# All input products and attention first, then the two later products as seven block products each

## The chip, the cores and the metric

The kernel runs on one core of a Trainium2 chip. The metric is the device time in microseconds (us) of one execution. Three runs of the kernel before took 407.26, 409.66 and 410.86 us; the median is 409.66.

## The reference, cut to what matters

Attention runs in chunks of 32 queries over a window of 16 keys to the left and 8 to the right plus 8 memory slots. Its output x goes through a gated layer:

```python
h = np.maximum(x @ w_in, 0.0)              # x: 4 x 768 x 512, w_in: 512 x 1024
u, v = h[..., :512], h[..., 512:]
v_n = (v - mean(v)) / np.sqrt(var(v) + 1e-6)
v_s = einsum('ts,bsd->btd', w_spatial, v_n) + b_spatial[None, :, None]   # w_spatial: 768 x 768
out = (u * v_s) @ w_out                    # w_out: 512 x 512
```

There are 4 batches of 768 tokens, 8 heads of 64. The host hands over w_in and w_out as 64-bit floats, which the kernel converts.

## The kernel before, in words

**Precision.** Every operand of a large product is held as a high part (rounded to fp32r) and a low part (the rest). A product is three matmuls: high by high, low by high, high by low (`group`, lines 478 to 480). All three add into one PSUM bank.

**Units.** A batch's 768 tokens are 6 attention units of 128 tokens (24 in all). For a unit, `burst` does 64 small matmuls for the scores and 64 for the weighted values (L342), DVE takes the maximum, subtracts and sums (L395, L399, L409), ScalarE (ACT) does the exponential (L404), TensorE (PE) turns the weights and the result (L426, L441), and ACT and DVE write x in two parts (L446, L450).

**The layer.** Three units make a half batch. For each half, `ffn_v` multiplies 3 token tiles by the v half of w_in (12 matmuls of 512 columns each) and normalises them: ACT relu, DVE statistics, GpSimd (POOL) power, DVE scaling, then ACT and DVE split the result. `ffn_u` makes 4 tiles of u (12 matmuls of 384 columns each). `spatial` multiplies by w_spatial: 8 groups per batch, each 18 matmuls of 384 columns, then DVE adds the bias (L577), POOL multiplies by u (L581), ACT and DVE split (L584, L588). `ffn_o` multiplies by w_out: 6 groups of 12 matmuls of 512 columns per batch, ACT copies (L613), SP stores.

**Order.** Every piece is an `op` of a class `Plan` with an engine, an estimated time, reads, writes and a rank. `Plan.order` simulates the engines with these estimates and writes down one fixed order for each engine; at run time each engine works through its order and waits on semaphores. In the kernel before, the attention of batch b+1 lies beside the products of batch b; DMA loads go out on SP's queue as soon as their buffer is free. At the start, `keep_warm` (L493) issues 12 matmuls of 512 columns whose result is not used.

Of the kernel before, what the change touches and what calls it, by code (L numbers as in the profile page):

```python
# [25 lines left out]
class Plan:  # L26
# [8 lines left out]
    def __init__(self, rings, loose, rate, landing, lat):  # L35
        self.rings, self.loose = rings, loose
        self.rate, self.landing, self.lat = rate, landing, lat
        self.ops, self.writer, self.readers, self.slots, self.newest = [], {}, {}, {}, {}

    def op(self, eng, us, fn, r=(), w=(), rank=0.0, mb=0.0, tail=0.0, after=None, alone=False):  # L40
# [20 lines left out]
        self.ops.append((eng, us, fn, deps, rank, mb, tail, held, begun, alone))  # L61
        return n

    def order(self):
# [8 lines left out]
        pipe = {e: self.landing for e in ENGINES}  # L73
        lone = 0.0
# [6 lines left out]
        out = []  # L81
        while len(out) < len(ops):
            best = None
            for e, ns in waiting.items():
                pick = None
                for n in ns:
                    t = max(free[e], ready[n], free["POOL"] if ops[n][9] else 0.0, lone if e == "POOL" else 0.0)
                    for s in ops[n][7]:
# [13 lines left out]
            _, us, _, _, _, mb, tail, held, _, alone = ops[n]  # L102
# [5 lines left out]
            if alone:  # L108
                lone = t + us
            if mb:  # L110
                pipe[e] = max(pipe[e], t + us) + mb / self.rate
                end[n] = pipe[e] + self.landing
            else:
                end[n] = t + us + tail
            self.start[n] = t
            out.append((t, n))
            for m in users[n]:
                left[m] -= 1
                if not left[m]:
                    ready[m] = max([end[d] + self.lat for d in ops[m][3]] + [self.start[d] for d in ops[m][8]])  # L120
                    waiting[ops[m][0]].append(m)
        return [n for _, n in sorted(out)]

    def emit(self):
        for n in self.order():
            self.ops[n][2]()
# [3 lines left out]
def tile_chunked_attention_gmlp(  # L130
# [30 lines left out]
    HT = S // 2  # L161
    NC = S // CH
# [11 lines left out]
    sizes = {"f": 4, "sx": 1, "pt": 1, "xt": 1, "st": 4, "big": 4, "x": 2, "vn": ST, "u": 2 * ND,  # L174
             "q": 1, "k": 1, "vm": 3, "mv": 1, "kT": 1, "p": 1, "xs": 1, "pT": 1}
    plan = Plan(sizes, {"f", "st", "big"}, rate=0.33, landing=2.0, lat=0.06)
# [11 lines left out]
    def pool(name, **kw):  # L188
# [3 lines left out]
    small = pool("small", bufs=3)  # L192
    sb = {name: pool(name, bufs=sizes[name]) for name in ("st", "big", "x", "vn", "u", "q", "k",
                                                         "kT", "p", "xs", "pT")}
    early_scope = ctx.enter_context(ExitStack())
    early = early_scope.enter_context(tc.tile_pool(name="early", bufs=1))
    ps = {name: pool(f"ps_{name}", bufs=sizes[name], space=PSUM) for name in ("f", "sx", "pt", "xt")}

    win_h = const.tile([P, KT, DF], F32R, name="win_h")
    win_l = const.tile([P, KT, DF], F32R, name="win_l")  # L200
    wsp_h = const.tile([P, ST, S], F32R, name="wsp_h")
    wsp_l = const.tile([P, ST, S], F32R, name="wsp_l")
    bias = const.tile([P, S], F32, name="bias")
    memT = const.tile([P, B, T, M], F32, name="memT")
    NV = sizes["vm"]
    vmain = const.tile([P, T, NV * UC, D], F32, name="vmain")
# [3 lines left out]
    warm = const.tile([P, 1], F32, name="warm")  # L210
    make_identity(nc, ident)
    nc.vector.memset(mhalf, -0.5)
# [9 lines left out]
    def load(dst, src_, w, rank, r=(), eng="SP", slow=1.0, us=0.45, seq=False):  # L222
# [5 lines left out]
        n = op(eng, us, lambda: e.dma_start(out=dst() if callable(dst) else dst, in_=src_), r=r, w=w, rank=rank, mb=mb,  # L228
               after=line.get(eng) if seq else None)
# [12 lines left out]
    def spot(name, g, shape):  # L242

        if (name, g) not in t_:
            if g in (1, 2):
                t_[name, g] = early.tile(shape, F32, name=f"{name}{g}")
            else:
                alloc(name, g, shape, F32)
        return t_[name, g]

    def key(name, g):
        return (name if g not in (1, 2) else "early", g, name)

    def load_qk(g, units=(0, 1), seq=True):
# [9 lines left out]
        ks = key("k", g)  # L264
        load(lambda: spot("q", g, [P, T, 2 * UT])[:, :, q0:q1],
             src(q, off + q0, [[S, P], [P * S, T], [1, q1 - q0]]), w=[key("q", g) + (u,)], rank=10.0 * i, slow=1.3, seq=seq)
        load(lambda: spot("k", g, [P, T, nk])[:, :, k0:k1],
             src(k, off - LEFT + k0, [[S, P], [P * S, T], [1, k1 - k0]]), w=[ks + (u,)], rank=10.0 * i, slow=1.3, seq=seq)
# [10 lines left out]
    def qk_keys(i, names="qk"):  # L279
        g, both = i // 2, [0, 1] if i == 1 else [0]  # L280
        return [key(n, g) + (u, *p) for n in names for u in both for p in ((), ("pad",))]
# [11 lines left out]
    def load_v(i, seq=True):  # L293
        b, c0 = i // UB, (i % UB) * UC
        n = UC
        v4 = v_of(i).rearrange("p t c d -> p t (c d)")
        for r in range(2):
            p0 = r * D
# [4 lines left out]
            def part(dst, src_, s, rows):  # L303
                load(dst, src_, w=[("vm", i, r, s)], rank=10.0 * i, slow=1.5, us=0.35, seq=seq)
# [10 lines left out]
    def v_keys(i):  # L315
        return [("vm", i, r, s) for r in range(2) for s in range(4)] + \
            [("mv", i // UB, r, t) for r in range(2) for t in range(T)]

    def load_mem(b, eng="SP", us=0.3, seq=True):
        for r in range(2):  # L320
            for t in range(T):
                load(vmain[r * D + CH:r * D + SLOT, t],
                     src(mem_v, (b * H + 2 * t + r) * M * D, [[D, M], [0, NV * UC], [1, D]]),
                     w=[("mv", b, r, t)], rank=10.0 * UB * b, eng=eng, slow=1.5, us=us, seq=seq)

    def prep(i, rank):
        b = i // UB

        def keys():
            a = alloc("kT", i, [P, T, UC + 1, SLOT], F32)  # L330
            nc.scalar.copy(a[:, :, :, 0:CH], k_of(i).rearrange("p t (c s) -> p t c s", s=CH))

        def mem():
            nc.gpsimd.tensor_copy(t_["kT", i][:, :, 0:UC, CH:SLOT],
                                  memT[:, b].unsqueeze(2).broadcast_to([P, T, UC, M]))
        op("ACT", act(T * (UC + 1) * CH), keys, r=qk_keys(i, "k"), w=[("kT", i)], rank=rank)
        op("POOL", 0.3, mem, r=["memT", ("kT", i)], w=[("kT", i, "m")], rank=rank)

    def burst(i, rank, split=False):

        def mm(o, w_, m):
            nc.tensor.matmul(o, w_, m, start=True, stop=True, skip_group_check=True)  # L342

        def go(what):
            if ("sx", i) not in t_:
                alloc("sx", i, [P, 2, 2, T, D], F32, psum=True)
            sx = t_["sx", i]
            tiles = [(t, c, r, slice(r * D, (r + 1) * D)) for t in range(T) for c in range(UC) for r in range(2)]
            if "s" in what:
                tq = q_of(i)  # L350
                kT = t_["kT", i].rearrange("p t c s -> p t (c s)")
# [8 lines left out]
        for what in (whole if split else [whole]):  # L360
            reads, writes = [], []
            us = 0.4
            if "s" in what:
                reads += qk_keys(i, "q") + [("kT", i), ("kT", i, "m")]
                writes.append(("sx", i, 0))
                us += 0.6
            if "a" in what:
                reads += [("pT", i - 1)] + v_keys(i - 1)
                writes.append(("sx", i, 1))
                us += 0.7  # L370
# [14 lines left out]
    def softmax(i, rank):  # L385
# [32 lines left out]
        op("DVE", dve(512) + 0.36, den, r=[("p", i)], w=[("rec", i)], rank=rank + 0.6)  # L418

    def flip(i, rank):  # L420
        if i < NU:
# [6 lines left out]
            def copy():  # L428
                nc.scalar.copy(alloc("pT", i, [P, T, P], F32), t_["pt", i])
            op("PE", 0.45, turn, r=[("p", i)], w=[("pt", i)], rank=rank, tail=0.25)  # L430
            op("ACT", act(512) - 0.04, copy, r=[("pt", i)], w=[("pT", i)], rank=rank)
        if i >= 1:
# [19 lines left out]
            op("PE", 0.45, turn_x, r=[("xs", j)], w=[("xt", j)], rank=rank - 0.5, tail=0.25)  # L452
            op("ACT", act(512) - 0.04, high, r=[("xt", j)], w=[("x", n, tt, "h")], rank=rank - 0.5)
            op("DVE", dve(512), low, r=[("xt", j), ("x", n, tt, "h")], w=[("x", n, tt, "l")], rank=rank - 0.5)
# [11 lines left out]
    def group(N, pairs, needs, first=(), get=None):  # L466
# [5 lines left out]
        for j, (pair, keys) in enumerate(zip(pairs, needs, strict=True)):  # L472
            def go(j=j, pair=pair):
# [7 lines left out]
            op("PE", 3e-3 * (0.4375 * N + 6.5), go, r=[*keys, *(first if j == 0 else ())], w=[("f", n)],  # L481
               rank=1e4 + seq[0], tail=0.25)
        seq[0] += 1
        return n

    def keep_warm(c, passes, rank):

        n = ("w", c)

        def go():  # L490
            o = alloc("f", n, [P, DH], F32, psum=True)
            for _ in range(passes):
                nc.tensor.matmul(o, win_h[:, c, DH:DH + P], win_h[:, c, DH:], start=True, stop=True)  # L493
        op("PE", passes * 0.43, go, r=[("win", c, 1, "h")], w=[("f", n)], rank=rank, tail=0.25)
# [4 lines left out]
    def ffn_v(b, tt):  # L499
        n_x, tok = 2 * b + tt // HU, slice((tt % HU) * P, (tt % HU + 1) * P)  # L500
        i = b * ST + tt
        rank = 45 + 1e-3 * seq[0]

        def pair(c):
# [3 lines left out]
                  [[("win", c, 1, s) for s in "hl"] + x_keys(b, tt) for c in range(KT)], [("vn", i)], lambda: alloc("vn", i, [P, 2, DH], F32R))  # L508
# [21 lines left out]
        def high():  # L530
            nc.scalar.copy(t_["vn", i][:, 0], t_["st", s])

        def low():
            a = t_["vn", i]
            nc.vector.tensor_tensor(a[:, 1], t_["st", s], a[:, 0].bitcast(F32), op=ALU.subtract)
        k_ = ("st", s)
        op("ACT", act(512), relu, r=[("f", n)], w=[k_], rank=rank)
        op("DVE", 1.05, stat, r=[k_], w=[("ve", i)], rank=rank)
        op("POOL", 0.6, power, r=[("ve", i)], w=[("rstd", i)], rank=rank)
        op("DVE", 0.43, norm, r=[("rstd", i)], w=[k_], rank=rank, alone=True)  # L540
        op("ACT", act(512), high, r=[k_], w=[("vn", i, "h")], rank=rank)
# [253 lines left out]
```

## Time and profile before

| | |
|---|---|
| median of three runs | 409.66 us |
| profiled execution, span from the first to the last instruction | 410.6 us |
| PE busy | 377.1 us, 92% |
| DVE, ACT, POOL busy | 201.2, 156.2, 99.3 us |
| DMA | 41.03 MB, mean 100 GB/s |

A matmul's time in a group is from its start to its modelled end; neighbours overlap, so the pace is read from the starts of successive matmuls in the timeline. The profile gives TensorE's granted clock in tenths; 1.00 is the upper of its two levels (2.4 GHz), 0.50 the lower (1.2 GHz). The execution that was profiled has no time of its own on the page beside its span.

### The profile page before, as it was taken

How to read it: one execution, taken by the hardware profiler on the slowest of the kernel's cores; microseconds unless marked ns; L12 is line 12 of the kernel's file. 1: busy time of each engine (PE TensorE's matmuls, PEld its weight loads, DVE VectorE, ACT ScalarE, POOL GpSimd, SP SyncE). 2: the span in 40 equal slices, each digit the busy share in tenths (PEclk: the TensorE clock that was granted, in tenths of full speed). 3: DMA queues.
4: the chain of work that ended last, by engine and by line, in shares of the span. 5: the costliest groups of instructions: out<-in, count | busy, mean ns of one | idle time of the engine just before them, and what ended most of it. 6: DMA issues, size and time to landing. Idle time of an engine off the chain costs nothing.

```text
span 410.6 us, 11090 instructions
## 1 busy us (share of the span) xinstructions
PE 377.1 (92%) x4824; PEld 336.2 (82%) x4824; DVE 201.2 (49%) x391; ACT 156.2 (38%) x277; POOL 99.3 (24%) x129
## 2 busy tenths in 40 slices
PE   1394899989999999989999999999999999999996
PEld 0263688879989887969997988989989989899895
DVE  0766787677736625665561631476331414424040
ACT  2645667376343324443424223344221123231212
POOL 5322359338302201011120120110120301103031
PEclk9996699999999999999999999999999999999999
DMA  7997734792343293320377332000002020000202
GB/s 183 249 253 206 237 125 133 199 283 83 85 148 127 57 242 105 92 93 7 106 149 209 116 110 77 2 2 2 3 0 77 2 77 2 0 0 2 77 2 77
DMA packets 35153, 41.03 MB, mean 100 GB/s; under 512 B 5216, under 2 KB 29664, under 8 KB 35104
## 3 DMA queue, kind: packets, MB, share of 16 engines
q1 hardware_dynamic: 34704, 40.05, 34.4%
q8 instruction: 38, 0.62, 0.7%
q0 software_dynamic: 256, 0.20, 0.4%
q14 instruction: 11, 0.09, 0.1%
q10 hardware_dynamic: 144, 0.07, 0.1%
HBM read 34.01 MB, written 6.29 MB: 98 GB/s over the span
## 4 chain that ended last, share of the span: by engine, by line
PE 73%; issue 7%; DMA 7%; DVE 3%; SPq 3%; POOL 3%; ACT 3%; POOLq 0%; ACTq 0%
PE f L478 21%; PE f L479 20%; PE f L480 20%; PE sx L342 7%; DMA big<-in_moe_w_in_dram 5%; SPq L228 3%; PE xt L441 2%; PE pt L426 2%; DMA big<-in_moe_w_out_dram 2%; POOL st L646 1%; DMA q<-in_q_dram 1%; ACT st L631 1%; DVE st L528 1%; ACT big L636 1%; DVE stats L516 0%
## 5 line engine op out<-in xcount | busy, mean ns | idle before, releaser
L478 PE MATMUL f<-wsp_h,vn 128*128 128x384 f32 x192 | 66.7, 348 | 0.0
L479 PE MATMUL f<-wsp_h,vn 128*128 128x384 f32 x192 | 64.7, 337 | 0.0
L480 PE MATMUL f<-wsp_l,vn 128*128 128x384 f32 x192 | 64.6, 336 | 0.0
L581 POOL TENSOR_TENSOR st<-st,u 128x384 f32<-128x384 f32 x32 | 33.2, 1037 | 123.9 <-DVE st L577 119.6
L478 PE MATMUL f<-x,win_h 128*128 128x384 f32 x128 | 44.6, 349 | 0.0
L577 DVE TENSOR_TENSOR st<-f,bias 128x384 f32<-128x384 f32 x32 | 17.8, 556 | 52.6 <-PE f L480 52.6
L479 PE MATMUL f<-x,win_l 128*128 128x384 f32 x128 | 43.2, 338 | 0.0
L480 PE MATMUL f<-x,win_h 128*128 128x384 f32 x128 | 43.2, 337 | 0.0
L584 ACT CAST big<-st 128x384 fp32r<-128x384 f32 x32 | 16.4, 513 | 67.7 <-POOL st L581 67.7
L524 POOL TENSOR_TENSOR rstd<-ve,mhalf 128x1 f32<-128x1 f32 x24 | 15.1, 628 | 111.3 <-DVE ve L520 98.9
L478 PE MATMUL f<-win_h,x 128*128 128x512 f32 x96 | 40.0, 417 | 1.6 <-issue 1.6
L478 PE MATMUL f<-wout,big 128*128 128x512 f32 (+1 forms) x100 | 39.1, 391 | 0.0
L480 PE MATMUL f<-wout,big 128*128 128x512 f32 (+1 forms) x100 | 38.6, 386 | 0.0
L479 PE MATMUL f<-wout,big 128*128 128x512 f32 (+1 forms) x100 | 38.6, 386 | 0.0
L479 PE MATMUL f<-win_h,x 128*128 128x512 f32 x96 | 38.5, 401 | 0.0
L480 PE MATMUL f<-win_l,x 128*128 128x512 f32 x96 | 38.4, 400 | 0.0
L478 PEld LDWEIGHTS f<-wsp_h,vn 128*128 128x128 f32 x192 | 36.1, 188 | 1.4
L479 PEld LDWEIGHTS f<-wsp_h,vn 128*128 128x128 f32 x192 | 36.2, 188 | 0.7
L480 PEld LDWEIGHTS f<-wsp_l,vn 128*128 128x128 f32 x192 | 36.1, 188 | 0.0
L516 DVE BATCH_NORM_STATS2 stats<-st 128x6 f32<-128x512 f32 x24 | 16.5, 689 | 32.8 <-ACT st L512 32.7
L342 PEld LDWEIGHTS sx<-kT,q 64*32 64x32 f32 x1536 | 17.3, 109 | 18.4 <-issue 8.4
L378 DVE TENSOR_TENSOR xs<-sx,rec 128x512 f32<-128x512 f32 x24 | 16.5, 687 | 32.2 <-PE sx L342 28.7
(67 smaller groups left out, 676.2 us busy)
## 6 DMA issues: line engine op xcount, KB each, us to landing
vmain<-in_v_dram SPq DMA_DIRECT2D x48, 128.0 KB
out_dram<-st SPq DMA_DIRECT2D x23, 256.0 KB
q<-in_q_dram SPq DMA_DIRECT2D x11, 512.0 KB
vmain<-in_v_dram SPq DMA_DIRECT2D x47, 96.0 KB
big<-in_moe_w_in_dram SPq DMA_DIRECT2D x8, 512.0 KB
k<-in_k_dram SPq DMA_DIRECT2D x7, 544.0 KB
k<-in_k_dram SPq DMA_DIRECT2D x4, 576.0 KB
big<-in_moe_w_spatial_dram SPq DMA_DIRECT2D x6, 384.0 KB
```

The costliest lines, as they stand in the source:

```text
L228: n = op(eng, us, lambda: e.dma_start(out=dst() if callable(dst) else dst, in_=src_), r=r, w=w, rank=rank, mb=mb, after=line.get(eng) if s ...
L342: nc.tensor.matmul(o, w_, m, start=True, stop=True, skip_group_check=True)
L378: nc.vector.tensor_tensor(xs.rearrange("p t r d -> p r t d"), t_["sx", i][:, :, 1], rec.rearrange("p t r -> p r t").unsqueeze(3).broadcast ...
L426: nc.tensor.transpose(a[:, t], p[:, t], ident)
L478: nc.tensor.matmul(o, lh, rh, start=(j == 0), stop=False)
L479: nc.tensor.matmul(o, ll, rh, start=False, stop=False)
L480: nc.tensor.matmul(o, lh, rl, start=False, stop=(j == len(pairs) - 1))
L516: nc.vector.bn_stats(stats, t_["st", s])
L524: nc.gpsimd.tensor_tensor(a, t_["ve", i], mhalf, op=ALU.pow)
L577: nc.vector.tensor_tensor(alloc("st", s_, [P, HT], F32), t_["f", n], bias[:, tok], op=ALU.add)
L581: nc.gpsimd.tensor_tensor(a, a, t_["u", i], op=ALU.mult)
L584: nc.scalar.copy(t_["g", i][:, 0, 0:HT], t_["st", s_])
```

## The change

What it does:

- **Two halves of the program.** Attention of all batches, `ffn_v` and `ffn_u` come first. The normalised v and u are no longer kept in SBUF: each tile is stored to buffers in DRAM (`vn_far`, `u_far`). In the second half they are loaded again, batch by batch (`near_v`, `near_u`); the loads of v wait for the end of attention, those of u for the last matmul group of the first half.
- **Seven block products.** `spatial` and `ffn_o` become calls of `product`, which cuts both operands in 2 x 2 blocks and makes seven block products instead of eight. The left operands' sums s1 to s4 are made by DVE for each batch, and each of the seven left operands is split by ACT and DVE. The right operands (w_spatial, w_out) get their seven sums once (`right_hand`). The bias of the first 384 positions enters as one more matmul of a group; POOL adds the difference for the other positions (`shift`). `ffn_o` of a batch runs between the products of the next batch's `spatial`. Its matmuls have 256 columns.
- **DMA.** A transfer is issued only once an older one has landed, so that at most 8 transfers and 1.75 MB (2.0 MB over the first 9 MB) are in flight. The memory values come in two loads and are copied to their places by POOL and DVE. The load order at the start differs.
- **PE.** `keep_warm` is gone; between 9 and 36 us of the plan's time, gaps are filled with matmuls of a constant. The planner's estimates change, one of them for DVE and POOL beside each other.
- **Last stores.** The last block's stores are halved, one half on SP's queue, one on ACT's.

```diff
+    def held_by(self, flight, mb, none):
+        window = self.window if sum(size for _, size in flight) > self.early[0] else self.early[1]
+        for back, (name, size) in enumerate(reversed(flight), 1):
+            mb += size
+            if back == 8 and window == self.window or mb > window:
+                return name
+        return none
...
+    def busy(k):
+        for _ in range(k):
+            nc.tensor.matmul(idle, ident, ident.unsqueeze(1).broadcast_to([P, 2, P]), start=True, stop=True)
...
+        op("SP", 0.45, lambda: transfer(nc.sync, vn_far[i // HU][:, i % HU], t_["st", s], P * DH * 4e-6), r=[k_],
+           w=[("vn_far", i // HU, i % HU)], rank=rank, mb=P * DH * 4e-6)
...
+        load(get, vn_far[i], w=[("vr", i)], r=["attended"] + [("vn_far", i, j) for j in range(HU)], rank=rank)
...
+        load(get, u_far[(b * 2 + dh) * 2 + th], w=[("ug", i, 0), ("ug", i, 1)],
+             r=[("u_far", i, j) for j in range(2)] + [("fin", n) for n in range(count[0])], rank=rank)
...
+    def product(kind, b, steps, halves, chunks, width, parts, N, right, right_keys, sum_eng, seed, done):
...
+                    for s in range(chunks):
+                        h, l_ = half(0)[:, s, cols], half(1)[:, s, cols]
+                        rh, rl = right(bi, 0, s), right(bi, 1, s)
+                        for x, y in ((h, rh), (l_, rh), (h, rl)):
...
+                s1 = total("s1", a21, a22, ALU.add, [*k21, *k22])
+                s2 = total("s2", s1[0], a11, ALU.subtract, [*s1[1], *k11])
...
+            blocks(name, left(*of), i, bank, name in ("p1", "p2", "p5"))
+            yield
...
+            def gate(x, dh, th):
+                u = ("ug", (b, dh, th))
+                def go():
+                    g = t_[u][:, p]
+                    nc.gpsimd.tensor_tensor(g, t_[st(x)], g, op=ALU.mult)
+                op("POOL", 1.3, go, r=[st(x)], w=[(*u, p)], rank=rank)
...
+        return product("s", b, ["p1", "p2", "p6", "p5", "p7", "p4", "p3"], [quarter(0, 0), quarter(0, 1), quarter(1, 0), quarter(1, 1)], HU, 2 * P, 2, HT,
...
+        return product("o", b, ["p1", "p6", "p5", "p7", "p4", "p3", "p2"], [quarter(1, 1), quarter(1, 0), quarter(0, 1), quarter(0, 0)], 2, HT, HU, HN,
...
+    load_mem()
...
     load_qk(0, (0,))
...
+    load_qk(0, (1,))
+    w_in_part(0, 1, 5.0 + 0, 2.0 + 0, "DVE")
+    w_in_part(1, 1, 5.0 + 1, 2.0 + 1, "DVE")
+    w_in_part(2, 1, 5.0 + 2, 2.0 + 2, "DVE")
+    w_in_part(3, 1, 5.0 + 3, 2.0 + 3, "DVE")
     load_v(0)
...
+    load_qk(1)
+    w_in_part(0, 0, 25.0 + 0, 15.0 + 0, "POOL")
     load_v(1)
...
+    w_in_part(1, 0, 25.0 + 1, 15.0 + 1, "POOL")
     load_v(2)
...
+    w_in_part(2, 0, 25.0 + 2, 15.0 + 2, "POOL")
+    w_in_part(3, 0, 25.0 + 3, 15.0 + 3, "POOL")
...
+            spatials.append(spatial(b))
+            for _ in range((1, 2, 2, 1)[b]):
+                next(spatials[b])
+        if b:
+            o = ffn_o(b - 1)
+            if b == B - 1:
+                for _ in range(6):
+                    next(o)
+                held = o
+            else:
+                next(o)
+                if b == B:
+                    for _ in held:
+                        pass
+                for _ in o:
+                    pass
+        if b < B:
+            for _ in spatials[b]:
+                pass
```

## Rows read from the trace of the kernel before

**Rows 1.** The head of the profile page: span, busy time of the engines, and the span in 40 slices of 10.3 us, PE's busy tenths and its granted clock in tenths.

```profile
span 410.6 us, 11090 instructions
PE 377.1 (92%) x4824; PEld 336.2 (82%) x4824; DVE 201.2 (49%) x391; ACT 156.2 (38%) x277; POOL 99.3 (24%) x129
...
PE   1394899989999999989999999999999999999996
...
PEclk9996699999999999999999999999999999999999
```

**Rows 2.** Busy time of each engine in four stretches (us from the start): PE, PEld (weight loads), DVE, ACT, POOL, each with its instructions; then PE's mean granted clock, the DMA engines' mean busy share, and GB/s.

```profile
0.00:50.00 50.00, 26.24 (x519) 19.71 (x523) 27.50 (x53) 24.47 (x41) 16.93 (x30) 0.86 0.89 223
36.00:48.00 12.00, 8.50 (x156) 6.61 (x156) 8.93 (x16) 6.39 (x11) 3.53 (x4) 0.51 0.65 182
50.00:400.00 350.00, 343.71 (x4272) 310.41 (x4272) 172.61 (x338) 129.38 (x231) 81.10 (x99) 1.00 0.28 83
50.00:250.00 200.00, 193.71 (x3191) 172.91 (x3191) 115.36 (x226) 87.82 (x155) 57.39 (x71) 1.00 0.46 131
210.00:220.00 10.00, 10.00 (x172) 8.37 (x171) 5.06 (x10) 2.98 (x6) 2.25 (x3) 1.00 0.99 203
```

**Rows 3.** PE's groups in the first 50 us, with the idle time ahead of each and what ended it: the unused matmuls of L493, and the weighted values of L342.

```profile
L493 PE MATMUL f<-win_h 128*128 128x512 f32 x12 | 5.7, 616 | 6.6 <-ACT win_h L649 6.6
L342 PE MATMUL sx<-vmain,pT 64*32 64x64 f32 x199 | 4.5, 283 | 7.7 <-issue 3.4 <-ACT pT L429 2.5 <-ACT st L631 1.8
```

**Rows 4.** Matmul groups of the whole span, shapes apart; each stands for one of the three lines 478 to 480, so the number of matmuls is three times the count.

```profile
L478 PE MATMUL f<-wsp_h,vn 128*128 128x384 f32 x192 | 66.7, 348 | 0.0
...
L478 PE MATMUL f<-x,win_h 128*128 128x384 f32 x128 | 44.6, 349 | 0.0
...
L478 PE MATMUL f<-win_h,x 128*128 128x512 f32 x96 | 40.0, 417 | 1.6 <-issue 1.6
...
L478 PE MATMUL f<-wout,big 128*128 128x512 f32 x92 | 36.9, 401 | 0.0
```

**Rows 5.** The timeline of PE near the end (start, duration, both in us): 384 columns, 512 columns, and then the first and the last of 15 successive matmuls of 256 columns.

```profile
396.94 0.34 PE L478 MATMUL f<-wsp_h,vn 128*128 128x384 f32 x1
...
397.81 0.34 PE L480 MATMUL f<-wsp_l,vn 128*128 128x384 f32 x1
...
399.21 0.39 PE L478 MATMUL f<-wout,big 128*128 128x512 f32 x1
...
400.38 0.39 PE L480 MATMUL f<-wout,big 128*128 128x512 f32 x1
...
405.16 0.28 PE L478 MATMUL f<-wout,big 128*128 128x256 f32 x1
...
406.84 0.28 PE L480 MATMUL f<-wout,big 128*128 128x256 f32 x1
```

**Rows 6.** The chain that ended last, pieces from 120 to 130 us (start, duration): the small matmuls of one attention unit, and four turns of each kind.

```profile
124.54 0.44 PE pt L426 x4
...
126.03 1.55 PE sx L342 x104
...
129.36 0.44 PE xt L441 x4
```

**Rows 7.** Groups of ACT, POOL and DVE over the whole span: the conversion of w_in, the softmax of a unit, the bias and the low parts.

```profile
L631 ACT ACTIVATE st<-big 128x512 f32<-128x512 f32 x12 | 8.0, 667 | 12.1 <-DMA big<-in_moe_w_in_dram 8.5 <-DMA big<-in_moe_w_out_dram 3.6
L649 ACT CAST win_h<-st 128x512 fp32r<-128x512 f32 x8 | 5.0, 622 | 3.5 <-POOL st L646 3.5
L687 ACT CAST wsp_h<-big 128x768 fp32r<-128x768 f32 x6 | 4.9, 832 | 0.0
L404 ACT ACTIVATE p<-p 128x512 f32<-128x512 f32 x24 | 15.2, 632 | 17.6 <-DVE p L399 17.5
L581 POOL TENSOR_TENSOR st<-st,u 128x384 f32<-128x384 f32 x32 | 33.2, 1037 | 123.9 <-DVE st L577 119.6 <-ACT big L584 4.3
L646 POOL TENSOR_TENSOR st<-st,big 128x512 uint32<-128x512 uint32 x12 | 16.5, 1375 | 32.6 <-DVE st L641 14.1 <-issue 6.4 <-ACT big L636 5.3
L654 POOL TENSOR_TENSOR win_l<-st,win_h 128x512 fp32r<-128x512 f32 x4 | 5.7, 1416 | 3.5 <-ACT win_h L649 2.0 <-DMA q<-in_q_dram 1.5
L577 DVE TENSOR_TENSOR st<-f,bias 128x384 f32<-128x384 f32 x32 | 17.8, 556 | 52.6 <-PE f L480 52.6
L399 DVE TENSOR_TENSOR p<-sx,mx 128x512 f32<-128x512 f32 x24 | 16.5, 689 | 5.9 <-PE sx L342 5.4
L588 DVE TENSOR_TENSOR big<-st,big 128x384 fp32r<-128x384 f32 x32 | 21.7, 679 | 18.4 <-ACT big L584 18.1
```

**Rows 8.** DMA: what was read and written over the span, from the page; and the stretch with hardly anything but a store of 256 KB in it, with the columns of the second group.

```profile
HBM read 34.01 MB, written 6.29 MB: 98 GB/s over the span
...
380.00:390.00 10.00, 10.00 (x50) 8.86 (x49) 0.56 (x1) 2.28 (x4) 0.55 (x1) 1.00 0.21 79
```

**Rows 9.** The last piece of the chain that ended last: the copy out of PSUM ahead of the last store.

```profile
407.15 0.37 ACT st L613
```

**Rows 10.** The timeline of POOL and DVE from 393 to 396 us (start, duration): one product by u, and two low parts, the first beside it and the second alone.

```profile
393.68 1.02 POOL L581 TENSOR_TENSOR st<-st,u 128x384 f32<-128x384 f32 x1 [0.54 <-DVE st L577]
...
393.72 1.39 DVE L588 TENSOR_TENSOR big<-st,big 128x384 fp32r<-128x384 f32 x1
...
395.27 0.56 DVE L588 TENSOR_TENSOR big<-st,big 128x384 fp32r<-128x384 f32 x1 [0.17 <-ACT big L584]
```

More of the change, by code (lines that the diff above doesn't have):

```diff
@@ L60, in op @@
         begun -= deps
-        self.ops.append((eng, us, fn, deps, rank, mb, tail, held, begun, alone))
+        self.ops.append((eng, us, fn, deps, rank, mb, tail, held, begun, alone, drag, shared))
         return n
@@ L101, in order @@
             (t, _, n), e = best
-            _, us, _, _, _, mb, tail, held, _, alone = ops[n]
+            if e == "PE" and self.idle and 9.0 < t < 36.0:
+                spare = int((t - max(free[e], 9.0) - 0.5) / 0.45)
+                if spare > 0:
+                    spares.append((max(free[e], 9.0), -spare))
+            _, us, _, _, _, mb, tail, held, _, alone, drag, shared = ops[n]
+            beside, pace = {"DVE": (free["POOL"] if shared else 0.0, 1.75), "POOL": (both, 1.4)}.get(e, (0.0, 1.0))
+            if beside > t:
+                us += min((beside - t) * (1 - 1 / pace), us * (pace - 1))
             for s in held:
@@ L161, in tile_chunked_attention_gmlp @@
     HT = S // 2
+    HN = H * D // 2
     NC = S // CH
@@ L191, in tile_chunked_attention_gmlp @@
     const = pool("const", bufs=1)
[L192 to L206, printed above, removed]
+    small = pool("small", bufs=8)
+    sb = {name: pool(name, bufs=sizes[name]) for name in ("st", "big", "uo")}
+    ps = {"f": pool("ps_f", bufs=sizes["f"], space=PSUM)}
+    far = pool("far", bufs=1, space=bass.MemoryType.DRAM)
+    vn_far = [far.tile([P, HU, DH], F32, name=f"vn_far{i}") for i in range(2 * B)]
+    u_far = [far.tile([P, 2, HT], F32, name=f"u_far{i}") for i in range(4 * B)]
+    wsp = const.tile([P, 7, 2, HU, HT], F32R, name="wsp")
+    bias = const.tile([P, HT], F32R, name="bias")
+    step = const.tile([P, HT], F32, name="step")
+    ones = const.tile([P, P], F32R, name="ones")
     ident = const.tile([P, P], F32, name="ident")
@@ new lines, in spread_mem, with spread @@
+    def spread_mem(i, eng, rank):
+        b, o = i // UB, (i % NV) * UC
+        for r in range(2):
+            rows = slice(r * D + CH, r * D + SLOT)
+            def spread(rows=rows, r=r):
+                to, of = vmain[rows, :, o:o + UC], memv[rows, b].unsqueeze(2).broadcast_to([M, T, UC, D])
+                ins = {"DVE": nc.vector, "POOL": nc.gpsimd}[eng].tensor_copy(to, of)
+                made.setdefault(("vmem", i % NV), []).append(ins.ins.name)
+            op(eng, 1.1 if eng == "POOL" else 1.25, spread, r=[("memv", r)], w=[("vmem", i % NV, r)], rank=rank)
@@ L480, in go @@
                 nc.tensor.matmul(o, lh, rl, start=False, stop=(j == len(pairs) - 1))
-            op("PE", 3e-3 * (0.4375 * N + 6.5), go, r=[*keys, *(first if j == 0 else ())], w=[("f", n)],
-               rank=1e4 + seq[0], tail=0.25)
+            op("PE", 3e-3 * (0.4375 * N + 6.5), go, r=[*keys, *(first if j == 0 else ())],
+               w=[("f", n), ("fin", n)], rank=1e4 + seq[0], tail=0.25)
         seq[0] += 1
         return n
[L486 to L494, printed above, removed]
     def x_keys(b, tt):
@@ new lines, in second_half, with third_part @@
+    def second_half():
+        if "op" not in sb:
+            attention.close()
+            for name in ("vr", "op", "sm"):
+                sb[name] = pool(name, bufs=sizes[name], side="right")
+            ps["y"] = pool("ps_y", bufs=sizes["y"], space=PSUM, side="right")
+    def third_part():
+        if "ug" not in sb:
+            ffn.close()
+            for name in ("ug", "ot"):
+                sb[name] = pool(name, bufs=sizes[name])
+            t_["wout"] = pool("wout", bufs=1).tile([P, 7, 2, 2, HN], F32R, name="wout")
@@ new lines, in from_f64, with split, high, low @@
+        if home:
+            return (lambda: t_[big][:, :, 1].bitcast(F32)), ("big", big)
+        return (lambda: t_["st", ("z", name)]), zk
+    def split(eng, n, dst, of, reads, writes, rank):
+        def high():
+            nc.scalar.copy(dst(0), of())
+        def low():
+            e = {"POOL": nc.gpsimd, "DVE": nc.vector}[eng]
+            e.tensor_tensor(dst(1), of(), dst(0).bitcast(F32), op=ALU.subtract)
+        op("ACT", act(n), high, r=reads, w=[(*w, "h") for w in writes], rank=rank)
+        op(eng, pool_(n) if eng == "POOL" else dve(n), low, r=[*reads, *[(*w, "h") for w in writes]], w=writes, rank=rank,
+           shared=eng == "DVE")
@@ new lines, in w_out_pair, with halves, dst @@
+    def w_out_pair(c, rank, load_rank):
+        def halves(z):
+            return lambda: z().rearrange("p (h n) -> p h n", h=2)
+        def dst(i, x):
+            third_part()
+            return t_["wout"][:, i, x, c]
+        (zu, ku), (zd, kd) = [from_f64(("wout", d), w_out[d * P:(d + 1) * P], 260.0, load_rank, True) for d in (c + 2, c)]
+        end = [("fin", n) for n in range(count[0])]
+        right_hand("wout", c, HN, halves(zu), halves(zd), [ku, *end], [kd, *end], dst, rank, "POOL", "DVE")
@@ new lines, in load_bias, with relative, high, low @@
+    def load_bias(rank):
+        raw = ("big", "bias")
+        def get():
+            t_[raw] = alloc("big", "bias", [P, 1024], U32).bitcast(F32)
+            return t_[raw][:, 0:S]
+        def relative():
+            nc.gpsimd.memset(t_[raw][:, S:S + P], 0.0)
+            for j in range(2):
+                nc.gpsimd.memset(t_[raw][CH * j:CH * j + 1, S:S + P], 1.0)
+            nc.gpsimd.tensor_tensor(step, t_[raw][:, HT:S], t_[raw][:, 0:HT], op=ALU.subtract)
+        def high():
+            nc.scalar.copy(bias, t_[raw][:, 0:HT])
+            nc.scalar.copy(ones, t_[raw][:, S:S + P])
+        def low():
+            b2 = bias[CH:CH + 1]
+            nc.vector.tensor_tensor(b2, t_[raw][CH:CH + 1, 0:HT], b2.bitcast(F32), op=ALU.subtract)
+        load(get, src(b_sp, 0, [[0, P], [1, S]]), w=[raw], r=[("wsp", 2, 6)], rank=rank, seq=True)
+        op("POOL", 1.6, relative, r=[raw], w=["step", (*raw, "d")], rank=rank)
+        op("ACT", 0.8, high, r=[raw, (*raw, "d")], w=["bias h"], rank=rank)
+        op("DVE", dve(HT), low, r=["bias h", raw], w=["bias"], rank=rank)
@@ new lines, in tile_chunked_attention_gmlp @@
+    for i in range(NU + 1):
+        attend(i, 10.0 * i, 1 <= i < UB)
+        j = i + 2
+        if i >= 1 and j < NU:
+            if j >= UB and j % UB < NK:
+                spread_keys(j, 10.0 * j)
+            if j >= UB and j % UB < NV:
+                spread_mem(j, "POOL", 10.0 * j)
+            load_v(j)
+        if i % 2 == 1 and i // 2 + 2 < NU // 2:
+            load_qk(i // 2 + 2)
+        if i - UB in (0, 4, 8):
+            w_sp_pair((0, 4, 8).index(i - UB), 10.0 * i + 15)
+        if i == UB + 11:
+            load_bias(10.0 * i)
```

529 lines of the change are left out of this document (327 added, 202 removed).

## Prediction

> **What bounds the kernel now.** I read the page's head and its slices first. PE is busy 377.1 of 410.6 us, no other engine over 49%, and PE's digits fall below 8 only in the first five slices [rows 1]. The windows then put numbers on it: from 0 to 50 us PE is busy 26.24 us, from 50 to 400 us 343.71 of 350 [rows 2]. So this is a PE-bound kernel with a poor start, and only two things can shorten it much: fewer PE cycles after 50 us, or a better first 50 us. The start loses 50 − 26.24 = 23.8 us idle, another 5.7 us to matmuls whose result nobody uses [rows 3], and half of the 8.50 busy us between 36 and 48 us, where the granted clock is 0.51, the lower level, after a stretch with gaps [rows 2]: 23.8 + 5.7 + 4.2 = 33.7 us.
>
> **PE's cycles.** Before, the w_spatial product has 3 x 192 = 576 matmuls of 384 columns [rows 4]. Pace from the starts of neighbours: five steps of 384 columns take 397.81 − 396.94, 0.174 us each; five of 512 take 1.17, 0.234 each; fourteen of 256 take 1.68, 0.120 each [rows 5]. After, per batch: 7 products x 2 parts x 3 chunks x 3 = 126, and 2 for the bias; four batches make 512. That is 64 x 0.174 = 11.1 us less. The w_out product has 24 x 12 = 288 of 512 columns (67.4 us); after, 4 x 7 x 3 x 2 x 3 = 504 of 256 (60.5 us): 6.9 us less. PE was never idle in that stage, so all **18.0 us** count. The danger is that a 256-column matmul has a weight load of its own; the fourteen steps were each a new weight load and still held 0.120.
>
> **The start.** Before u can be made, the loads up to the last w_in part must land: memory 0.13 MB, q and k of two units 1.08, w_in for v 2.10, values of three units 1.38, next q and k 1.11, w_in for u 2.10: 7.9 MB. At the 223 GB/s of the first 50 us [rows 2] that is 35.4 us. The last part's conversion then takes two ACT passes, two DVE passes, a POOL addition, an ACT cast and a POOL subtraction; with 0.67 twice, two DVE passes of up to 0.69, 1.38, 0.62 and 1.42 [rows 7] about 6 us. So PE can run dense from about 41 us. By then it has done three attention units at 1.55 + 0.44 + 0.44 = 2.43 us [rows 6], a fourth unit's scores (0.8) and three v tiles of 12 x 0.234 = 2.8: 16.5 us. Loss 24.5 instead of 33.7, a gain of **9.2 us**. Bounds: nothing, if the fillers stand ahead of late data; 13 us, if the loads run at 250 GB/s (223 at a share of 0.89). I take the computed value, as its rate is this stage's own. The fillers count nothing while they lie in idle time; they should hold the clock at its upper level where the rows show 0.51.
>
> **The first half after that** costs nothing by my account, and this is what covers it. Per half batch PE has 3 x 2.43 for attention, 3 x 2.8 for v and 4 x 12 x 0.174 = 8.4 for u: 24 us. One unit's chain is scores 1.55, two DVE passes 0.69, exponential 0.63, turn 0.44, a copy of about 0.6, some 4.6 us; three take 14, so attention stays ahead. DVE's 201.2 us lose in this half the work on spatial (17.8 + 21.7, [rows 7]) and the low part of v (24 x 0.69), leaving 145 us in some 217. POOL gets 32 us for w_spatial's sums and low parts and 30 to 50 us of copies of memory values (no row: bounds 0.3 and 2.4 us each, nearest a POOL pass over 768 elements); its queue is not full. SP gets 48 stores more in line with the loads: a load behind a store waits for that store's ACT or DVE step. What they hold up next is a unit's q, k or v; one half batch of attention ahead is the cover, and a stall here would show as PE idle at the scores.
>
> DMA is the tight one. Read 34.0 MB plus 12.6 MB of stores [rows 8], less 7.9 MB by 41 us, is 38.7 MB until the half ends: PE needs 24 x 2.43 + 288 x 0.234 + 384 x 0.174 = 192.5 us, less 16.5, so 176 us, or 220 GB/s. In 50 to 250 us the engines gave 131 GB/s at a share of 0.46, 285 when full; stores alone 79 at 0.21, 376 [rows 8]; the worst slice 203 at 0.99 [rows 2]. 26 MB at 250 to 285 and 12.6 MB at 376 take 125 to 138 of 176 us. Price: nothing to +15 us (all of it at 203 GB/s: 191 us). I take 0, by the stretch of 200 us rather than the slice of 10.
>
> **The hand-over.** The first v block of the second half needs a load of 0.8 MB, two of them 1.6 MB, after the last unit: 5.8 us at 270, some 3 to land (407.52 to 410.6 is what the last store takes, [rows 1, 9]), then a cast of 0.83 [rows 7] and a low part of 0.95: under 10 us. In line on PE meanwhile is the last v tile and four u tiles: 2.8 + 8.4 = 11.2 us. Cost 0; without that cover 10 us.
>
> **The second half's new work on DVE.** From 0.556 (384) and 0.689 (512) [rows 7] one more element costs 1.04 ns: 768 elements 0.955, 256 elements 0.42. Per batch w_spatial needs 4 sums + 7 low parts at 0.955 and 8 passes at 0.556: 15.0 us; w_out 11 x 0.955 + 9 x 0.42 = 14.3. That is 29.3 us beside 22.3 + 15.1 = 37.4 of PE, 78%. POOL has 10 passes of 1.04 per batch. The trace shows that the two hinder each other: a low part took 1.39 beside POOL's product and 0.56 alone [rows 10]. At 0.83 for every POOL pass DVE comes to 37.6 of 37.4; the mean over 32 (0.679, [rows 7]) says a third to half of it. So PE should stay the bound with short waits where w_spatial and w_out change over and at the end, where w_out's last six products are alone: there p6 waits for a multiply, two sums, a cast and a low part, some 4.3 us behind 3.1 + 2.2 + 2.2 us of PE work. I take **+5 us** (one at each of three changes, two at the end); bounds 0 and 16 (DVE's 150 us and 10 for w_out's preparation in place of PE's 150, and 6 at the changes).
>
> The Trainium skill, in "SBUF — State Buffer", section "Who interferes with whom", says that a DVE instruction with two SBUF inputs and a GpSimd instruction that reads SBUF exclude each other for a whole instruction. The 1.39 agrees. By that rule taken for every pass the sum would carry the upper bound of 16.
>
> **The tail.** An addition of 0.42 replaces a copy of 0.37 [rows 9], and the stores are half as large: 0 within 0.3 us.
>
> **Sum.** 410.6 − 18.0 − 9.2 + 5 = 388.4 us. The median of the three runs lies 0.9 below the span, and a run's time has nothing else shown around it, so I set 387.5.
>
> **Rivals.**
>
> 1. *DVE becomes the bound of the second half.* For it: 37.6 against 37.4 us at the full price of [rows 10], in queues with a fixed order. Against: the mean of 0.679. Time: waits of 16 instead of 5, and half the start's gain: 387.5 + 11 + 4.6 = 403. Range 396 to 408.
> 2. *Slower: DMA bounds the first half.* Place: q, k and v loads in one line with 12.6 MB of new stores, at most 8 in flight. Price: each 10 GB/s below 220 costs about 8 us. Slower than before means 27 us lost, 38.7 MB in 203 us: it decides at 191 GB/s. At 170 GB/s: 228 us, +52, about 439; at 185, 421. For it: a slice at 203. Against: no full slice under 203, 285 over the long stretch. The Trainium skill ("SBUF — State Buffer", "A bandwidth-pool intuition that's wrong (but worth ruling out)") holds HBM to be the usual end-to-end bottleneck; here a mean of 98 GB/s over the span shows that it was not before the change.
> 3. *Weight loads bound the 256-column products.* PEld's loads are shown at 0.188 us; at that pace 504 x 0.068 = 34 us more, 421. Against: fourteen steps at 0.120 [rows 5].
> 4. *Better still.* Start at its upper bound, no waits, and half of the 6.3 us idle in 50 to 400 gone: 387.5 − 3.8 − 5 − 3 = 376.
>
> That the change does less than it says is only possible where an order leaves PE waiting, which is rival 1.
>
> **Chances.** Forecast (378 to 396) 0.70; rival 1 0.12; rival 2 0.08; rival 3 0.03; rival 4 0.07. The range from 376 to 404 holds the forecast, most of rival 1 and half of rival 4, about 0.82. Three runs of before spread over 0.9%, so 1% (405.6 to 413.8) is what counts as no change. Faster: 0.70 + 0.07 + 0.09 of rival 1 = 0.86; same: 0.03 of rival 1, 0.02 of rivals 2 and 3 = 0.05; slower: 0.09.
>
> **What would show it.** PE's cycles: 171 per line of 384 columns from w_spatial and 168 of 256 from w_out, at 0.120 between starts. Start: busy above 30 us of the first 50 without the fillers, clock 1.00 throughout. First half: DMA near 200 GB/s and hardly any PE idle ahead of the small attention matmuls. Second half: DVE about 80% busy, PE waits on its low parts of 5 us together. Wrong would be long PE waits for v loads between 50 and 217 us (rival 2), a pace of 0.188 (rival 3), or DVE above 95% with PE under 90% (rival 1).

## The result, and the profile after

The changed kernel took 376.78 us (median of 4 runs, 375.94 to 377.45) against 408.46 us, a ratio of 0.925 with a 95% interval of 0.9191 to 0.9309. Measured once more beside the experiments it was 376.59 us (6 runs), ratio 0.9239 (0.9211 to 0.9266). 387.5 was forecast, 376 to 404 as the range: the direction was right, the time lies 0.8 us inside the range's lower edge, 11 us under the forecast and below the forecast's own band of 378 to 396. Ratios leave out executions that lie over 1.5% above the fastest of the same kernel.

The head of the page after and its slices of 9.35 us answer to [rows 1]:

```profile
span 374.1 us, 11859 instructions
PE 357.9 (96%) x4996; PEld 329.4 (88%) x4996; DVE 282.5 (76%) x472; ACT 188.8 (50%) x336; POOL 159.4 (43%) x158
...
PE   2998999999989999999999999999999999999996
...
PEclk9999999999999999999999999999999999999999
```

The start fills after one slice, and once the clock is up it does not fall. In the first 13 us the row shows 1.00, but the durations show the lower level: the 64 small matmuls of a unit's scores take 1.18 us there and 0.86 later, both in the changed kernel:

```profile
10.81 1.18 PE L411 MATMUL sx<-kmain,q 64*32 64x64 f32 x64
23.72 0.86 PE L411 MATMUL sx<-kmain,q 64*32 64x64 f32 x64
```

The kernel before has such a stretch too, up to about 24 us (1.18 us for the same 64 matmuls at 6.98 us), where [rows 1] show the upper level. The same kernel in stretches (columns as in [rows 2]): the first 50 us, the rest of the first half, the second half, the end.

```profile
0.00:50.00 50.00, 40.30 (x786) 32.05 (x786) 37.93 (x73) 29.13 (x50) 26.90 (x34) 1.00 0.95 245
50.00:217.00 167.00, 164.76 (x3171) 145.13 (x3171) 114.33 (x237) 85.20 (x150) 70.32 (x79) 1.00 0.69 208
217.00:360.00 143.00, 142.54 (x957) 142.10 (x956) 122.44 (x151) 69.19 (x127) 62.21 (x46) 1.00 0.35 118
360.00:374.10 14.10, 10.35 (x88) 10.12 (x86) 7.83 (x14) 5.29 (x11) 0.00 (x0) 1.00 0.35 112
```

Of the first 50 us the filling matmuls took 11.98:

```profile
0.00:50.00 50.00, 11.98 (x44) 8.94 (x44) 1.00 0.95 245
```

The chain of the second half (start, duration) shows the two paces, each over 18 matmuls, and the last addition ahead of the last stores, which answers to [rows 9]:

```profile
224.94 3.12 PE f L704 x18
...
254.51 2.10 PE f L704 x18
...
370.38 0.42 DVE ot L814
```

Dividing, 3.12 / 18 is 0.1733 us for 384 columns, 2.10 / 18 is 0.1167 for 256. Now the 36.5 us between the spans can be split:

| | forecast | measured |
|---|---|---|
| PE's cycles in the two products | −18.0 | −19.7 (0.120 forecast, 0.1167 found) |
| the first 50 us | −9.2 | −12.0 (33.7 lost before; 9.7 idle + 12.0 filler now) |
| PE idle from 50 us to its last matmul | +5 | −3.6 (6.3 before; 2.24 + 0.46 now) |
| after the last matmul | 0 | +0.3 |

That is −35.0. Of the 1.5 us left, some 0.4 are the lower level at the very start, which the table does not count (half of PE's busy time there without the unused matmuls, an estimate, is 1.9 us before and 1.5 now); the rest is not assigned to any row.

The split holds for the two profiled executions. The one of the kernel before was a long one: its span of 410.6 us compares with 404.3 to 411.4 in the 37 other executions of it on record, whose medians on three occasions were 406.3, 407.5 and 408.1. The medians of the times differ by 31.7 us, not 36.5. The prediction took the median to lie 0.9 us below the span; on record an execution takes 1.7 to 2.2 us more than its own span. The second half of the changed kernel hardly varies (149.05 us, and 148.99 when it was run again), so up to 5 us of what the table gives to the start and to idle time may belong to that one execution.

### The profile page after: what moved, and what is told of

Its sections match the earlier page's. It is cut to its first block, busy times and chain, and to the rows that moved or that the text cites. A ratio compares the mean times of both kernels' runs of the same rounds, so it can differ in the third digit from the quotient of the medians.

```text
span 374.1 us, 11859 instructions
## 1 busy us (share of the span) xinstructions
PE 357.9 (96%) x4996; PEld 329.4 (88%) x4996; DVE 282.5 (76%) x472; ACT 188.8 (50%) x336; POOL 159.4 (43%) x158
## 4 chain that ended last, share of the span: by engine, by line
PE 88%; DVE 5%; ACT 2%; issue 2%; DMA 1%; SPq 0%; ACTq 0%; DVEq 0%
PE y L704 22%; PE f L704 15%; PE f L553 12%; PE f L554 11%; PE f L555 11%; PE sx L411 9%; PE xt L515 3%; PE pt L499 3%; DMA k<-in_k_dram 1%; DVE op L682 1%; DVE st L867 1%; PE idle L251 1%; DVE st L866 1%; DVE sm L665 0%; PE y L698 0%
## 5 line engine op out<-in xcount | busy, mean ns | idle before, releaser
L704 PE MATMUL y<-wsp,op 128*128 128x384 f32 x288 | 52.6, 336 | 0.0
L760 POOL TENSOR_TENSOR ug<-st,ug 128x384 f32<-128x384 f32 x24 | 35.8, 1508 | 35.8 <-DVE st L752 31.6
L704 PEld LDWEIGHTS y<-wsp,op 128*128 128x128 f32 x288 | 50.1, 188 | 0.0
L704 PE MATMUL f<-wsp,op 128*128 128x384 f32 x216 | 39.4, 336 | 0.0
L682 DVE TENSOR_TENSOR op<-sm,op 128x768 fp32r<-128x768 f32 x32 | 35.7, 1121 | 4.8 <-ACT op L679 4.6
L704 PEld LDWEIGHTS f<-wsp,op 128*128 128x128 f32 x216 | 37.6, 188 | 0.0
L704 PE MATMUL y<-wout,op 128*128 128x256 f32 x288 | 35.9, 280 | 0.5 <-DVE op L682 0.5
L704 PEld LDWEIGHTS y<-wout,op 128*128 128x128 f32 x288 | 34.8, 188 | 0.9 <-DVE op L682 0.8
L679 ACT CAST op<-sm 128x768 fp32r<-128x768 f32 x32 | 26.3, 839 | 12.7 <-DVE sm L665 9.0
L390 POOL COPY vmain<-memv 8x1024 f32<-8x1024 f32 x22 | 23.5, 1075 | 11.5 <-PE sx L411 9.2
L704 PE MATMUL f<-wout,op 128*128 128x256 f32 x216 | 27.0, 280 | 0.0
```

Of the source, the lines that this page charges most:

```text
L390: ins = {"DVE": nc.vector, "POOL": nc.gpsimd}[eng].tensor_copy(to, of)
L679: nc.scalar.copy(half(0), of())
L682: nc.vector.tensor_tensor(half(1), of(), half(0).bitcast(F32), op=ALU.subtract)
L704: nc.tensor.matmul(o, x, y, start=first and m == 1 and not (seed and bank == "y"), stop=m == 3 * chunks, skip_group_check=True)
L760: nc.gpsimd.tensor_tensor(g, t_[st(x)], g, op=ALU.mult)
```

## The experiments

Ratios are to the kernel before on the same chip; 0.01 of it is 4.1 us. The base is the changed kernel run again among them:

> The changed kernel unchanged, as the base for the other runs: 0.925 of the kernel before, as measured.

0.9239 (0.9211 to 0.9266).

**Does PE's work count one for one?**

```diff
-                    for s in range(chunks):
+                    again = 2 if name == "p2" and kind == "s" else 1
+                    for s in list(range(chunks)) * again:
```

> The changed kernel with the matmuls of the second block product of the w_spatial product done twice (so this product is counted twice in the output): 8 x 9 = 72 more matmuls of 384 columns, the order of all engines the same. My theory, PE bounds the second half and its cycles count one for one: 72 x 0.174 = 12.5 us more, 389 us. Rival, DVE (81% busy there) sets the pace and PE has slack: 0 to 5 us more.

0.9535 (0.9499 to 0.9571): 12.1 us more than the base, 13.5 more by the span (387.6 against 374.1; 12.8 against the base's 374.8). The second half alone shows it best: from the first matmul of the two products to the end of the last one the traces have 149.05 us in the changed kernel, 148.99 when it was run again, and 161.39 here, 12.3 more. One for one. The same line with kind "o":

> The same for the w_out product: its last block product of each batch done twice, 4 x 3 x 6 = 72 more matmuls of 256 columns. My theory: 72 x 0.120 = 8.6 us more, 385 us. Rival 3 of the prediction, weight loads at 0.188 us bound these products: 13.5 us more. Rival, DVE sets the pace where w_out's products run: under 3 us more.

0.9392 (0.9353 to 0.9432): 6.3 us more, give or take 2; by the span (382.6) 7.8 to 8.5. The second half takes 156.84 us, 7.8 more; 72 x 0.1167 is 8.4. The weight loads' 13.5 and DVE's "under 3" both lie outside. So an eighth block product's matmuls would cost their cycles, all of them in the w_spatial product and nine tenths or more in the other.

**What the start is made of.** In the three runs of the changed kernel that follow the second half takes 149.0 to 149.1 us; what they cost lies ahead of it. Without the waits of the throttle (`if wait:` to `if False:`), the order of all engines the same:

> The changed kernel without the waits that hold a transfer back until an older one has landed; the planner still counts on them, so the order is the same. Theory A, the start was gained by transfers that land in turn: without it the values of the second and third unit land late, PE idles in the first 50 us, and 5 to 10 us of the 12 us gained there are lost (382 to 387 us). Theory B, the new order of loads alone does it: within 1 us (376 to 378).

0.9364 (0.933 to 0.9397), 5.1 us more. Without the filler (`self.idle(-n)` to `pass`):

> The changed kernel without the filling matmuls between 9 and 36 us. Theory A, they hold the granted clock at its upper level: without them a stretch of the first 50 us shows 0.5, and the time grows by 2 to 5 us (379 to 382). Theory B, they only stand in the way of data that is there: 0 to 1 us less.

0.9299 (0.9254 to 0.9345), 2.5 us more, with an interval of about 2 on that. One effect is in the durations of the same 64 matmuls: without the fillers they are at the lower level up to about 28 us, with them up to 13.

```profile
23.59 1.19 PE L411 MATMUL sx<-kmain,q 64*32 64x64 f32 x64 [1.30 <-ACT kmain L396]
30.90 0.86 PE L411 MATMUL sx<-kmain,q 64*32 64x64 f32 x64 [0.22 <-DVE xs L451]
```

The windows of the two runs, from 30 to 40 us, first without the throttle:

```profile
30.00:35.00 5.00, 1.37 (x67) 0.95 (x49) 2.27 (x6) 4.34 (x8) 3.37 (x4) 0.86 1.00 216
35.00:40.00 5.00, 4.35 (x60) 3.49 (x60) 3.22 (x6) 0.00 (x0) 0.48 (x2) 0.50 0.21 69
```

then without the filler:

```profile
30.00:35.00 5.00, 2.84 (x137) 2.18 (x130) 3.35 (x7) 4.20 (x8) 3.12 (x3) 1.00 0.98 231
35.00:40.00 5.00, 4.27 (x18) 3.41 (x18) 3.37 (x6) 1.42 (x4) 2.15 (x2) 0.50 0.40 105
```

In both PE is idle for some 2 to 4 us and then works at the lower level (0.50), as the kernel before did from 36 to 48 us [rows 2]. Where the first gap comes from is seen in PE's timeline, at the values of the second unit. Without the throttle:

```profile
31.04 0.33 PE L411 MATMUL sx<-vmain,pT 64*32 64x64 f32 x13
35.65 0.65 PE L411 MATMUL sx<-vmain,pT 64*32 64x64 f32 x29 [4.28 <-issue]
```

and in the changed kernel:

```profile
31.04 0.33 PE L411 MATMUL sx<-vmain,pT 64*32 64x64 f32 x13
32.35 0.74 PE L411 MATMUL sx<-vmain,pT 64*32 64x64 f32 x51 [0.98 <-issue]
```

PE stands after the thirteenth of 64 matmuls. In the changed code the waits for the values sit on the first of them, so it is not the data that is late, as theory A had it; the profile names nothing that PE waits for there (the last section comes back to this). Without both:

> The changed kernel without the throttle's waits and without the filling matmuls. If both act alone, the sum of the two single runs' losses; if the filler only pays where data is late, more than the sum.

0.9328 (0.9282 to 0.9373), 3.6 us more: less than the two losses added, so neither expectation fits. What it shows is more useful:

```profile
0.00:50.00 50.00, 30.53 (x724) 24.10 (x727) 36.68 (x69) 28.12 (x48) 26.15 (x33) 1.00 0.94 243
65.00:70.00 5.00, 3.01 (x135) 2.15 (x134) 2.27 (x7) 1.80 (x3) 1.10 (x2) 0.98 0.47 127
70.00:75.00 5.00, 5.00 (x23) 4.05 (x19) 3.13 (x6) 1.13 (x3) 0.00 (x0) 0.68 0.63 202
```

With neither, PE is busy 30.5 us in the first 50, against the 40.3 − 12.0 of the changed kernel; but up to about 28 us its matmuls run at the lower level, as without the fillers. With such time counted half, an estimate from the windows, PE does about 25 us of work in the first 50 here, 27 in the changed kernel and 14 in the kernel before. A longer gap and the lower level come after 65 us. That points to what all these runs share, the order of loads and work, as the source of some 10 of the 12 us. The throttle alone in the kernel before points the same way:

```diff
+        if wait:
+            tc.add_manual_dep(ins.ins, wait, mybir.DependencyInfo(mybir.DependencyClass.Sync, mybir.DependencyReason.DATA), reason="pace")
```

> The kernel before with the throttle alone: at most 8 transfers and 1.75 MB (2.0 over the first 9 MB) in flight, order of all engines as before. If the throttle is what mends the start, part of the 12 us shows here: 4 to 8 us less than before (401 to 405). If the load order does it, within 2 us of before, or slower, as loads of later units wait in line.

1.0087 (1.006 to 1.0115): 3.6 us slower. PE's list of waits (engine, line, what for: us, times, longest) says why:

```profile
PE sx L357 <- POOL kT L349: 21.6, 2, 21.1
```

The waiting loads on GpSimd's own queue held up the copy behind them. With the throttle off that queue:

> The kernel before with the throttle on SP's and ACT's transfers only. With the throttle on all, the eight loads of memory values on GpSimd's queue waited in line and held up the copy that the first scores need (first scores at 21 us instead of 7). Theory A, the throttle lets the values of the second and third unit land in turn: 3 to 6 us less than before (403 to 406). Theory B, in the old order of loads it has nothing to give: within 2 us of before.

0.9995 (0.9964 to 1.0027): nothing. Theory B.

**Is DVE or POOL near its limit in the second half?** Each of POOL's passes twice on the same data:

```diff
                     nc.gpsimd.tensor_tensor(g, t_[st(x)], g, op=ALU.mult)
+                    nc.gpsimd.tensor_tensor(g, t_[st(x)], g, op=ALU.mult)
...
+                    for _ in range(2 if eng == "POOL" else 1):
```

> The changed kernel with each of GpSimd's passes of the second half (the product by u, the added bias difference) done twice on the same data, so the output is multiplied and shifted twice: 38 more POOL passes of 384 elements. Theory A, POOL's passes hold up DVE's and DVE stands close to being the bound (81% busy, low parts 1.12 to 1.23 us where 0.955 was computed): DVE goes to about 90%, low parts longer by 0.1 us or more, and PE waits 3 to 10 us (380 to 387). Theory B, the queues between DVE and PE are deep enough: DVE's passes get longer, the time stays within 2 us.

0.9813 (0.9766 to 0.986): 23.5 us more, far beyond both. Two stretches, and the shares of the chain of waits from 215 us on:

```profile
240.00:250.00 10.00, 10.00 (x60) 10.00 (x59) 6.27 (x9) 0.83 (x1) 9.69 (x9) 1.00 0.01 2
250.00:260.00 10.00, 6.06 (x32) 5.54 (x31) 6.59 (x6) 3.90 (x7) 8.23 (x7) 0.83 0.00 1
```

```profile
by line: PE y L704 16.0%; POOL st L768 12.7%; DVE op L682 12.4%; PE f L704 11.7%; POOL ug L760 9.6%; POOL ug L761 9.3%; DVE sm L665 5.9%; issue 4.5%; ACT op L679 3.5%; DVE st L752 2.5%; DVE wout L892 1.9%; DVE st L593 0.5%; DVE stats L581 0
```

POOL fills up (9.69 of 10), DVE is at 6.3 and waits; 31.6% of the chain is POOL's own passes. What stops PE is POOL's queue at the end of a w_spatial product: its products by u are the next w_out product's operands. A part of the loss is the clock, which falls after such stops (0.83 in the second stretch). Then the reverse, `shift` left out:

> The changed kernel without the addition of the bias difference (the second 384 positions get the first 384 bias values): 14 POOL passes and 2 DVE passes fewer in the second half. If DVE's waits for POOL cost the changed kernel time, 2 to 6 us less; if PE never waits for them there, DVE's low parts get shorter (toward 0.955 us) and the time stays within 1 us.

0.9292 (0.9243 to 0.9341): no gain; the interval overlaps the base's, and the second half takes 148.86 us against 149.05. The groups of DVE's low parts from v and of POOL's products by u, in the changed kernel over the whole span:

```profile
L760 POOL TENSOR_TENSOR ug<-st,ug 128x384 f32<-128x384 f32 x24 | 35.8, 1508 | 35.8 <-DVE st L752 31.6 <-DVE st L766 4.2
...
L766 POOL TENSOR_TENSOR st<-st,step 128x384 f32<-128x384 f32 x14 | 17.7, 1272 | 41.2 <-ACT st L746 29.7 <-DVE st L752 11.5
...
L682 DVE TENSOR_TENSOR op<-vr,op 128x768 fp32r<-128x768 f32 x12 | 14.8, 1234 | 2.7 <-ACT op L679 2.6
```

and without the shift, from 217 us on:

```profile
L682 DVE TENSOR_TENSOR op<-vr,op 128x768 fp32r<-128x768 f32 x11 | 10.5, 953 | 4.4 <-ACT op L679 4.3
```

Without `shift` beside it, the low part takes the 0.955 us that was worked out from [rows 7]; with it 1.234. POOL's product by u takes 1.508 where it took 1.037 in the kernel before. Both engines slow down; what `shift` does to DVE costs the changed kernel no time.

**Is DMA near its limit in the first half?** Every tile of v and u stored a second time:

```diff
-        op("SP", 0.45, lambda: transfer(nc.sync, vn_far[i // HU][:, i % HU], ...
+        op("SP", 0.45, lambda: [transfer(nc.sync, t[i // HU][:, i % HU], t_["st", s], P * DH * 4e-6) for t in (vn_far, vn_two)], ...
```

> The changed kernel with every tile of v and u stored twice in the first half, the second time to a buffer that nobody reads: 12.6 MB more, 56 more transfers on SP's queue, each counted by the throttle. Rival 2's mechanism, DMA close to the bound in the first half (208 GB/s at a share of 0.69): the share rises to 0.9 or more and PE idles, 5 to 25 us more (382 to 402). My theory, a third of the share is free: under 3 us more.

0.9406 (0.9329 to 0.9483): 6.8 us more, with an interval of about 3.

```profile
50.00:217.00 167.00, 157.09 (x3112) 136.44 (x3109) 106.80 (x222) 79.71 (x143) 67.62 (x75) 0.98 0.84 260
```

My "under 3" fell. The engines carried 260 GB/s, well over the 203 of the slice that I had taken as the pessimist's rate, but PE was idle for 9.9 us of the stretch instead of 2.2, at a mean share of only 0.84: loads came late in single places while the mean still left room. The longest wait, 2.67 us, is for a softmax on ACT, and ACT stood behind a load of k:

```profile
70.23 0.72 ACT L398 COPY kmain<-k 128x640 f32<-128x640 f32 x1 [6.14 <-DMA k<-in_k_dram]
```

Another 5.4 us are stops that the profile puts down to nothing, most of them of the kind of the last section. The second half is unchanged (149.00 us).

**The last stores** (`if b == B - 1 and x == "r1":` to `if False:`):

> The changed kernel with the last three stores whole, all on SP's queue. My prediction priced the halving at 0 within 0.3 us: no difference. Rival, the smaller halves on two queues land earlier: 0.5 to 1.5 us more here.

0.9225 (0.9187 to 0.9262) against 0.9239: no difference.

## Why the prediction was right, and where it was off

- **PE's cycles (−18.0).** Right in mechanism and close in size; the two runs with a block product done twice show that the matmuls left out count. The 256-column pace was read from the last fourteen steps of the kernel before, which ran at 0.120 against 0.1167 in the products: 1.7 us.
- **The start (−9.2).** Right in its steps. The last part of w_in for u began its conversion at 34.72 us (35.4 worked out) and u's matmuls began at 41.82 (41 worked out):

```profile
34.72 0.69 ACT L857 ACTIVATE st<-big 128x512 f32<-128x512 f32 x1 [0.94 <-DMA big<-in_moe_w_in_dram]
```

```profile
41.82 0.34 PE L553 MATMUL f<-x,win_h 128*128 128x384 f32 x1
```

  The 2.8 us beyond are work that I had not counted ahead of 41 us, if the profiled execution of before is taken as it is. The fillers act by the clock, but not where I said: without them and without the throttle the stretch from 36 to 48 us is at the upper level too. What they do is raise the clock some 15 us earlier, and only some 2 us hang on it. The stores were 56, not 48; their bytes were counted right.
- **"I take +5 us (one at each of three changes, two at the end)".** This is the term that was mis-sized. PE's waits in the whole changed kernel:

```profile
PE sx L411 <- ACT kmain L396: 6.8, 1, 6.8
...
PE xt L515 <- issue: 1.4, 1, 1.4
...
PE y L704 <- DVE op L682: 0.5, 1, 0.5
```

  The changes cost nothing and the end 0.5. DVE was somewhat busier than the 80% that I named (122.44 of 143 us, 86%), and still PE did not wait; what I added for waits at the changes had no row under it. The order has the operands ready, and the run without `shift` shows that relief for DVE brings nothing. The price of DVE meeting POOL came out in the band given, "a third to half" of 0.83: the low parts of the run without `shift` take 57.5 us from 217 us on against 63.1 in the base, 0.40 for each of the 14 passes left out. That was luck, as the mean it was read from gives (0.679 − 0.56) / 0.83, a seventh. "The 1.39 agrees" is too strong as well: that low part ended 0.41 us after POOL's product, where one that had waited for all of it would have needed its 0.56 [rows 10].
- **Not forecast:** the idle time from 50 us on fell from 6.3 to 2.7 us; I had carried the 6.3 over unchanged.
- **"POOL has 10 passes of 1.04 per batch."** They took 1.27 to 1.51. I priced only what POOL does to DVE, not the reverse. It cost nothing here, but POOL's passes done twice show that its queue is a bound not far off; what more work on DVE would cost no run shows.
- **Rivals.** Rival 2 did not come about (208 GB/s in the first half, PE idle 2.2 us), but the tiles stored twice put it nearer than my 125 to 138 of 176 us did. Rival 3 is excluded by the pace and by w_out's block product done twice. Rival 1 needs DVE as the bound; PE waited 0.5 us for it. Rival 4 (376) is what happened, nearly to the term, and it had been given a chance of 0.07: the range held the time because half of this rival had been counted into it, and by 0.8 us only.

## What to carry to other kernels

Where one engine is 99% busy in a stage, cycles taken from it can be counted one for one, and new work on the others is free until the first of their queues fills; look for that queue in passes that are last before the next stage, not in the mean busy share. Before adding a lump for "waits at the changes", find a row that such a wait would come from. A limit on transfers in flight was worth 5 us with the new order of loads and nothing with the old one; put on the wrong queue, it stopped the copy that stood behind it there.

## What the runs showed that was not expected

PE stops in the middle of a run of matmuls whose data is there, for nothing that the profile names: 0.98 us at one place in the changed kernel and 4.28 at the same place without the throttle, where the DMA engines' share is 0.95 and 1.00. The traces say more. Without the 44 filling matmuls PE stops at another place of the work:

```profile
32.27 0.79 PE L411 MATMUL sx<-vmain,pT 64*32 64x64 f32 x57
35.73 0.43 PE L411 MATMUL sx<-vmain,pT 64*32 64x64 f32 x7 [2.67 <-issue]
```

That is after the 57th matmul of the unit's values instead of the 13th, so 44 matmuls further on. Counted over all that PE issued, both stops stand after the 473rd matmul, and so do those without the throttle and without both. Later stops come after the 727th, 854th, 980th, 1106th, 1612th and 1992nd, which are 126 or 127 apart or a multiple of that. The page of the changed kernel lists a queue of the program's own instructions:

```profile
q8 instruction: 39, 0.64, 0.8%
```

These are 39 transfers of 16 KB for PE's 4996 matmuls, one for each 128. In the changed kernel and the ten later runs of it or of its variants, 41 stops of 0.3 us or more are put down to nothing by the profile; ahead of 40 of them, a transfer of this queue had landed 1.2 to 1.7 us before PE went on. Ahead of the stop of 0.98 us it ran from 29.32 to 31.14 us, ahead of that of 4.28 us from 32.69 to 34.01. So PE most likely waits for the next piece of its program, which crosses the same DMA engines as the data, and the throttle is worth most of its 5 us by letting that piece through. No run moved this alone, so it is not shown by experiment.

Which of the reordered loads or pieces of work brings the rest of the start's 12 us stays open: throttle and filler alone and together account for 2.5 to 5.1. No run has the two halves without the seven block products either, so the idle time that went after 50 us is not assigned to a part of the change.
